# Attention feeding an MLP on one core: q and k loaded by casting DMA in six-token runs, with a drained first batch and a new load order

## The chip, the cores and the metric

The kernel runs on one core of a Trainium2 chip. The metric is the device time of one execution in microseconds (us). The profile of an execution gives each engine's instructions: TensorE (PE, and PEld for its weight loads), VectorE (DVE), ScalarE (ACT), GpSimd (POOL) and the queue of SyncE (SPq) that issues DMAs. PEclk is the clock that TensorE was granted, as a share of full speed. PSUM holds TensorE's results; to evacuate is to copy them out of it. A pair's step is the time from its first scores matmul to that of the next pair. The page's span is 1.6 to 2.1 us shorter than the time of the same run; where I subtract milestones of two traces, I use spans.

## The reference, cut to what matters

```python
# q, k, v: (8, 8, 576, 64) float32: batch, head, sequence, head_dim
scores = 0.125 * q @ k^T + slope[h] * (-(i - j))       # only where 0 <= i - j < 128
x = (softmax(scores) @ v).transpose(0, 2, 1, 3).reshape(4608, 512)
h = x @ w_in                                           # 512 x 2048
out = (h * clip(h + 3, 0, 6) / 6) @ w_out              # 2048 x 512
```

The kernel works through 32 head pairs (four to a batch, pair 0 to pair 31). For each it transposes q and k, makes the scores, exponentiates, masks, multiplies by v, normalizes and transposes back into `xT`. The MLP (called MoE in the code) follows in 288 "units": 144 up units (one 128x512 piece of h) and 144 down units, each of four matmuls of 512 columns. A token block's up units can start when all pairs of the batches it touches have come back. They are put between the steps of later pairs, to fill TensorE.

## The kernel before

Only TensorE's order is fixed by the program. The order on the other engines is chosen when the kernel is built, and in the traces VectorE and GpSimd then work through it in that order (below, copies whose data had landed at 5.8 and 7.5 us run at 20.3 us, behind another instruction).

```python
ps_tp = ...tile_pool(name="ps_tp", bufs=2, space=PSUM)   # one tag "tp": q, k and back share two buffers
...
def load_pair(got, b, hp):              # batch 0; float32, 256 B runs, from SyncE
    for nm, src in srcs:                # q, k, v
        for h in (2 * hp, 2 * hp + 1):
            nc.sync.dma_start(out=got[nm][:, 0:4, h, :],
                              in_=src[b, h, 0:512, :].rearrange("(t p) d -> p t d", p=128))
            ...
def cast_all(got, b):                   # batches 1 to 7: GpSimd casts q, k, v to bf16
    ...
def transposes(g):
    b, hp = divmod(g, NP)
    for src, nm in ((qbuf[b % 2], "qT"), (kbuf[b % 2], "kT")):
        tp = ps_tp.tile([128, SP], BF16, tag="tp", name="tp")
        for j in range(NQ):             # five 128x128 blocks
            nc.tensor.transpose(tp[:, ts(j, 128)], src[:, j, ts(hp, 128)], ident)
        t = qkt.tile([128, SP], BF16, tag=nm, name=nm)
        nc.vector.tensor_copy(out=t, in_=tp)
...
with tc.manual_schedule(engines={mybir.EngineType.PE}):
    prepare(0)
    transposes(0)
    for g in range(G + 1):              # fill(n): up to n MoE units
        scores_diag(g);  prepare(g + 1);  fill(2)
        values(g - 1, (0, 1, 2));         fill(1)
        values(g - 1, (3, 4));            fill(1)
        scores_off(g);                    fill(1)
        transposes(g + 1);                fill(1)
        back(g - 1);                      fill(2)
    fill(len(units))
```

(Guards for the first and last pair are cut.) w_in is loaded at pair 1's preparation and w_out at pair 3's, both by casting DMAs from GpSimd.

The softmax here doesn't subtract the row's maximum and nothing guards it: scores larger than these inputs give would overflow.

Of the kernel before, what the change touches and what calls it, by code (L numbers as in the profile page):

```python
# [18 lines left out]
def kernel(  # L19
# [38 lines left out]
    loads = ctx.enter_context(tc.tile_pool(name="loads", bufs=4))  # L58
# [3 lines left out]
    small = ctx.enter_context(tc.tile_pool(name="small", bufs=4))  # L62
# [5 lines left out]
    ps_tp = ctx.enter_context(tc.tile_pool(name="ps_tp", bufs=2, space=bass.MemoryType.PSUM))  # L68
# [3 lines left out]
    qbuf = [held.tile([128, NQ, H * D], BF16, name=f"qbuf{i}") for i in range(2)]  # L72
    kbuf = [held.tile([128, NQ, H * D], BF16, name=f"kbuf{i}") for i in range(2)]
    vbuf = [held.tile([128, NQ, H, W], BF16, name=f"vbuf{i}") for i in range(2)]
    p4buf = [held.tile([128, 2, 128], BF16, name=f"p4buf{i}") for i in range(2)]

    srcs = (("qf", q), ("kf", k), ("vf", v))

    def new_loads():
        return {nm: loads.tile([128, NQ, H, D], FP32, tag="ld", name=nm) for nm, _ in srcs}  # L80

    def load_pair(got, b, hp):
        for nm, src in srcs:
            for h in (2 * hp, 2 * hp + 1):
                nc.sync.dma_start(out=got[nm][:, 0:4, h, :],
                                  in_=src[b, h, 0:512, :].rearrange("(t p) d -> p t d", p=128))
                nc.sync.dma_start(out=got[nm][:LAST, 4, h, :], in_=src[b, h, 512:S, :])  # L87

    def load_all(got, b):
        for nm, src in srcs:  # L90
            for j in range(NQ):
                n = min(128, S - j * 128)
                nc.sync.dma_start(
                    out=got[nm][:n, j, :, :],
                    in_=src[b, :, ds(j * 128, n), :].rearrange("h p d -> p h d"))

    got0 = new_loads()
    for hp in range(NP):
        load_pair(got0, 0, hp)
# [10 lines left out]
    for i in range(2):  # L110
        nc.vector.memset(vbuf[i][:, :, :, D:W], 1.0)
        nc.vector.memset(vbuf[i][64:128, 4, :, 0:D], 0.0)
        nc.vector.memset(qbuf[i][64:128, 4, :], 0.0)
        nc.vector.memset(kbuf[i][64:128, 4, :], 0.0)
        nc.vector.memset(p4buf[i], 1.0)

    def load_weights_in():
        for g in range(4):
            nc.gpsimd.dma_start(
                out=w_in_sb[:, :, ts(g, 512)],  # L120
                in_=moe_w_in[:, ts(g, 512)].rearrange("(k p) f -> p k f", p=128))
# [7 lines left out]
    def cast_pair(got, b, hp, eng):  # L129
        for nm, dst in (("qf", qbuf[b % 2]), ("kf", kbuf[b % 2])):  # L130
            s = got[nm].rearrange("p j h d -> p j (h d)")
            eng.tensor_copy(out=dst[:, 0:4, ts(hp, 128)], in_=s[:, 0:4, ts(hp, 128)])  # L132
            eng.tensor_copy(out=dst[:LAST, 4, ts(hp, 128)], in_=s[:LAST, 4, ts(hp, 128)])
        hs = slice(2 * hp, 2 * hp + 2)
        vb = vbuf[b % 2]
        eng.tensor_copy(out=vb[:, 0:4, hs, 0:D], in_=got["vf"][:, 0:4, hs, :])
        eng.tensor_copy(out=vb[:LAST, 4, hs, 0:D], in_=got["vf"][:LAST, 4, hs, :])

    def cast_all(got, b):
        for nm, dst in (("qf", qbuf[b % 2]), ("kf", kbuf[b % 2])):  # L140
            s = got[nm].rearrange("p j h d -> p j (h d)")
            nc.gpsimd.tensor_copy(out=dst[:, 0:4, :], in_=s[:, 0:4, :])
            nc.gpsimd.tensor_copy(out=dst[:LAST, 4, :], in_=s[:LAST, 4, :])
        vb = vbuf[b % 2]
        nc.gpsimd.tensor_copy(out=vb[:, 0:4, :, 0:D].rearrange("p j h d -> p (j h) d"),
                              in_=got["vf"][:, 0:4, :, :].rearrange("p j h d -> p (j h) d"))
        nc.gpsimd.tensor_copy(out=vb[:LAST, 4, :, 0:D], in_=got["vf"][:LAST, 4, :, :])
# [3 lines left out]
    def transposes(g):  # L151
        b, hp = divmod(g, NP)
        for src, nm in ((qbuf[b % 2], "qT"), (kbuf[b % 2], "kT")):
            tp = ps_tp.tile([128, SP], BF16, tag="tp", name="tp")
            for j in range(NQ):
                nc.tensor.transpose(tp[:, ts(j, 128)], src[:, j, ts(hp, 128)], ident)  # L156
            t = qkt.tile([128, SP], BF16, tag=nm, name=nm)
            nc.vector.tensor_copy(out=t, in_=tp)  # L158
            st[g, nm] = t
# [75 lines left out]
    def back(g):  # L235
        b, hp = divmod(g, NP)
        avs = st[g, "avs"]
        tp = ps_tp.tile([128, SP], BF16, tag="tp", name="tp")
        for j in range(NQ):
            nc.tensor.transpose(tp[:, ts(j, 128)],  # L240
                                avs[:, j, :, :].rearrange("p e d -> p (e d)"), ident)
        nc.vector.tensor_copy(out=xT[:, hp, ds(b * S, S)], in_=tp[:, 0:S])  # L242
        done[0] = g + 1
# [33 lines left out]
    units = []  # L277
    for nt in range(n_nt + 1):
        for step in range(16):
            if nt < n_nt:  # L280
                units.append((nt, moe_up, step))
            if nt > 0:
                units.append((nt, moe_down, step))
    at = [0]

    def fill(n):
        for _ in range(n):
            if at[0] == len(units):
                return
            nt, fn, step = units[at[0]]  # L290
            if fn is moe_up and done[0] < NP * (min((nt * NT + NT - 1) // S, B - 1) + 1):
                return
            fn(nt if fn is moe_up else nt - 1, step)
            at[0] += 1

    G = B * NP
    got = {0: got0}

    def prepare(g):
        b, hp = divmod(g, NP)  # L300
        if b == 0:
            cast_pair(got[0], 0, hp, nc.vector)
            if hp == 1:
                load_weights_in()
            if hp == 3:
                load_weights_out()
        elif hp == 0:
            cast_all(got[b], b)
        if hp == 1 and b + 1 < B:
            got[b + 1] = new_loads()  # L310
            load_all(got[b + 1], b + 1)

    with tc.manual_schedule(engines={mybir.EngineType.PE}):
        prepare(0)
        transposes(0)
        for g in range(G + 1):
            if g < G:
                scores_diag(g)
            if g + 1 < G:
                prepare(g + 1)  # L320
            fill(2)
            if g > 0:
                values(g - 1, (0, 1, 2))
            fill(1)
            if g > 0:
                values(g - 1, (3, 4))
            fill(1)
            if g < G:
                scores_off(g)
            fill(1)  # L330
            if g + 1 < G:
                transposes(g + 1)
            fill(1)
            if g > 0:
                back(g - 1)
            fill(2)
        fill(len(units))
# [30 lines left out]
```

## Time and profile before

| | before |
|---|---|
| time, median of the first 3 runs | 418.05 us (417.54 to 421.3) |
| first scores matmul (pair 0) | 18.8 us |
| pair 4's scores | 63.7 us |
| first up matmul | 69.2 us |
| pair 9's scores | 103.2 us |
| step of a pair, pairs 10 to 31, mean | 9.99 us |
| span (profiled run, 419.74 us) | 417.7 us |

These are the lines of the page that matter: engine totals (busy us, share, instructions), then busy tenths in 40 slices of the span, for TensorE, its granted clock and the DMA engines.

```profile
span 417.7 us, 7115 instructions
PE 338.9 (81%) x2739; PEld 175.2 (42%) x2784; DVE 201.5 (48%) x438; ACT 198.5 (48%) x355; POOL 145.1 (35%) x217
...
PE   0141618878999899989998999899899999999985
PEclk9999999998999999999999999999999999999999
DMA  8989799997157989898470000001000000101011
```

The first six slices (63 us) are mostly empty on TensorE, while DMA is nearly full. After the tenth slice TensorE is the limit. The timeline (start, duration, engine, line, operation, output from inputs, count, idle time before it and what ended it) shows how the first stage ends:

```profile
62.30 0.84 PE L156 MATMUL tp<-ident,kbuf 128*128 128x128 bf16 x5 [4.07 <-POOL kbuf L142]
...
63.73 0.61 PE L168 MATMUL sc<-qT,kT 64*128 64x128 bf16 x8
...
69.19 2.60 PE L253 MATMUL hps<-xT,w_in_sb 128*128 128x512 bf16 x7 [0.22 <-issue]
```

The k transposes of pair 4 (batch 1) wait for GpSimd's cast of batch 1. Pair 3's back-transposes stand behind them in TensorE's order, and the first up unit needs pair 3. In the second stage, the transposes of a pair look like this:

```profile
209.00 0.44 PE L156 MATMUL tp<-ident,qbuf 128*128 128x128 bf16 x5
...
209.28 0.44 PE L156 MATMUL tp<-ident,kbuf 128*128 128x128 bf16 x5
209.48 0.49 DVE L158 COPY qT<-tp 128x640 bf16<-128x640 bf16 x1 [1.26 <-PE tp L156]
```

k's transposes start right after q's, while q's evacuation on VectorE has not begun.

### The profile page before, as it was taken

To read this page: it belongs to the slowest core of one execution; us is meant where nothing else is said; L and a number is where in the kernel's file an instruction comes from. 1 tells how busy PE (TensorE), PEld (TensorE's weight loads), DVE (VectorE), ACT (ScalarE), POOL (GpSimd) and SP (SyncE) were. 2 spreads that over 40 slices of the span, in tenths; PEclk is the share of its full clock that TensorE was granted. 3 is DMA by queue.
4 is the path that set the end of the run, shared out by engine and by line. 5 is a ranking of instruction groups with operands and counts; after the bars stand their busy time and mean duration, and the time that the engine had idled before them with its cause. 6 is when DMAs were issued, how large, how long until landed. Compare 5 with 4: busy or idle time off the path is not lost.

```text
span 417.7 us, 7115 instructions
## 1 busy us (share of the span) xinstructions
PE 338.9 (81%) x2739; PEld 175.2 (42%) x2784; DVE 201.5 (48%) x438; ACT 198.5 (48%) x355; POOL 145.1 (35%) x217
## 2 busy tenths in 40 slices
PE   0141618878999899989998999899899999999985
PEld 0021415445444444444454444444444444444432
DVE  3341614675455555555555555555555454344400
ACT  0240414675655565555565655556565534443400
POOL 3070464458657427342752374222222200000000
PEclk9999999998999999999999999999999999999999
DMA  8989799997157989898470000001000000101011
GB/s 134 195 148 199 151 198 197 209 201 135 49 132 166 179 176 166 161 186 152 116 163 25 27 26 27 27 27 39 32 31 27 27 25 30 48 25 52 25 70 55
DMA packets 122481, 42.40 MB, mean 101 GB/s; under 512 B 113744, under 2 KB 117840, under 8 KB 122448
## 3 DMA queue, kind: packets, MB, share of 16 engines
q1 hardware_dynamic: 118224, 37.76, 44.3%
q0 software_dynamic: 4224, 4.19, 6.2%
q8 instruction: 21, 0.34, 0.4%
q14 instruction: 12, 0.10, 0.1%
HBM read 36.70 MB, written 9.44 MB: 110 GB/s over the span
## 4 chain that ended last, share of the span: by engine, by line
PE 46%; DVE 15%; ACT 14%; issue 11%; DMA 8%; SPq 4%; POOL 1%; DVEq 0%; POOLq 0%; ACTq 0%
PE ops L267 22%; PE hps L253 13%; ACT r L257 8%; DMA vf<-in_v_dram 6%; DVE g L258 5%; DVE avs L231 4%; DVE osb L274 3%; ACT pd L173 3%; PE tp L156 2%; PE sc L168 2%; PE av L222 2%; PE sc L189 2%; ACT p4buf L202 2%; SPq L87 2%; DMA kf<-in_k_dram 2%
## 5 line engine op out<-in xcount | busy, mean ns | idle before, releaser
L258 DVE SCALAR_TENSOR_TENSOR g<-r,hps 128x512 bf16<-128x512 f32 x144 | 99.0, 687 | 117.0 <-ACT r L257 116.9
L253 PE MATMUL hps<-xT,w_in_sb 128*128 128x512 bf16 x535 | 144.4, 382 | 10.5 <-DVE xT L242 5.3
L267 PE MATMUL ops<-w_out_sb,g 128*128 128x512 bf16 x572 | 145.2, 379 | 5.6 <-DVE osb L274 3.1
L257 ACT ACTIVATE r<-hps,bias 128x512 f32<-128x512 f32 x144 | 99.2, 691 | 96.8 <-PE hps L253 93.9
L267 PEld LDWEIGHTS <-g 128*128 128x128 bf16 x576 | 53.6, 98 | 70.0 <-issue 15.1
L176 POOL TENSOR_SCALAR_AFFINE_SELECT pd<-pd 128x512 bf16<-128x512 bf16 x64 | 39.8, 644 | 96.9 <-ACT pd L173 96.9
L253 PEld LDWEIGHTS <-w_in_sb 128*128 128x128 bf16 x576 | 49.8, 98 | 49.9 <-issue 4.1
L204 POOL TENSOR_SCALAR_AFFINE_SELECT po<-po 128x512 bf16<-128x512 bf16 x64 | 40.4, 634 | 79.0 <-ACT po L199 75.7
L199 ACT ACTIVATE po<-sc,bias_o 128x512 bf16<-128x512 f32 x64 | 44.0, 687 | 39.3 <-PE sc L193 39.3
L173 ACT ACTIVATE pd<-sc,bias_d 128x512 bf16<-128x512 f32 x64 | 40.5, 683 | 43.1 <-PE sc L168 43.1
L222 PE MATMUL av<-vbuf,po 128*128 128x65 bf16 x256 | 26.1, 201 | 15.4 <-DVE avs L231 15.3
L158 DVE COPY qT<-tp 128x640 bf16<-128x640 bf16 x32 | 15.7, 492 | 35.9 <-PE tp L156 35.8
L156 PE MATMUL tp<-ident,kbuf 128*128 128x128 bf16 x160 | 16.4, 239 | 20.0 <-DVE kbuf L132 15.9
L231 DVE TENSOR_TENSOR avs<-av,rc 128x384 bf16<-128x384 f32 x64 | 31.4, 491 | 2.0
L156 PE MATMUL tp<-ident,qbuf 128*128 128x128 bf16 x160 | 16.2, 238 | 19.5 <-DVE qbuf L132 15.2
L222 PEld LDWEIGHTS <-po 128*128 128x128 bf16 x256 | 18.9, 102 | 29.3 <-DVE avs L231 29.0
L225 PE MATMUL av<-vbuf,pd 128*128 128x65 bf16 x256 | 25.0, 201 | 0.0
L156 PEld LDWEIGHTS <-qbuf 128*128 128x128 bf16 x160 | 12.1, 105 | 26.2 <-DVE qbuf L132 15.5
L225 PEld LDWEIGHTS <-pd 128*128 128x128 bf16 x256 | 20.0, 101 | 7.2 <-issue 0.8
L156 PEld LDWEIGHTS <-kbuf 128*128 128x128 bf16 x160 | 11.4, 106 | 21.6 <-DVE kbuf L132 16.9
L202 ACT ACTIVATE p4buf<-sc,bias_d 128x64 bf16<-128x64 f32 x64 | 20.2, 315 | 0.0
L274 DVE COPY osb<-ops 128x512 f32<-128x512 f32 x18 | 12.3, 685 | 16.0 <-PE ops L267 16.0
(46 smaller groups left out, 231.8 us busy)
## 6 DMA issues: line engine op xcount, KB each, us to landing
out_dram<-osb SPq DMA_DIRECT2D x36, 256.0 KB, 2.0
qf<-in_q_dram SPq DMA_DIRECT2D x28, 256.0 KB, 4.9
kf<-in_k_dram SPq DMA_DIRECT2D x28, 256.0 KB, 5.1
vf<-in_v_dram SPq DMA_DIRECT2D x28, 256.0 KB, 4.9
w_in_sb<-in_moe_w_in_dram POOLq DMA_DIRECT2D x4, 512.0 KB, 10.4
w_out_sb<-in_moe_w_out_dram POOLq DMA_DIRECT2D x4, 512.0 KB, 10.1
qf<-in_q_dram SPq DMA_DIRECT2D x15, 128.0 KB, 5.3
kf<-in_k_dram SPq DMA_DIRECT2D x15, 128.0 KB, 4.8
```

Of the source, the lines that this page charges most:

```text
L156: nc.tensor.transpose(tp[:, ts(j, 128)], src[:, j, ts(hp, 128)], ident)
L173: nc.scalar.activation(out=pd[:, e, :, :].rearrange("p j c -> p (j c)"), in_=sc[:, e, :], func=ACT.Exp, bias=bias_d[:, h:h + 1], scale=scale)
L176: nc.gpsimd.affine_select(out=pd[:, e, :, :], in_=pd[:, e, :, :], pattern=[[0, 4], [1, 128]], channel_multiplier=-1, base=0, compare_op=AL ...
L199: nc.scalar.activation(out=po[:, e, :, :].rearrange("p j c -> p (j c)"), in_=sc[:, e, :], func=ACT.Exp, bias=bias_o[:, h:h + 1], scale=scale)
L204: nc.gpsimd.affine_select(out=po[:, e, :, :], in_=po[:, e, :, :], pattern=[[0, 4], [-1, 128]], channel_multiplier=1, base=-1, compare_op=A ...
L222: nc.tensor.matmul(av[:, i, e, :], lhsT=po[:, e, qt - 1, :], rhs=vb[:, qt - 1, h, :], start=True, stop=False)
L225: nc.tensor.matmul(av[:, i, e, :], lhsT=d, rhs=vb[:, qt, h, :], start=(qt == 0), stop=True)
L231: nc.vector.tensor_tensor(out=st[g, "avs"][:, qts[0]:qts[0] + nq, :, :], in0=av[:, 0:nq, :, 0:D], in1=rc[:, 0:nq, :, :].to_broadcast([128, ...
L253: nc.tensor.matmul(hps, lhsT=w_in_sb[:, ks, ts(ms, 128)], rhs=xT[:, ks, ts(nt, NT)], start=(ks == 0), stop=(ks == n_ks - 1))
L257: nc.scalar.activation(out=r6, in_=hps, func=ACT.Relu, bias=bias3[:, 0:1], scale=1.0 / 6.0)
L258: nc.vector.scalar_tensor_tensor(out=gts[nt][:, ms, :], in0=r6, scalar=1.0, in1=hps, op0=ALU.min, op1=ALU.mult)
L267: nc.tensor.matmul(ops[nt, sub], lhsT=gts[nt][:, ms, ts(sub, 128)], rhs=w_out_sb[:, ms, :], start=(ms == 0), stop=(ms == n_ms - 1))
```

## The change

Its intent: fewer and larger DMA packets for q and k, no casts of them, and MoE work that starts as soon as batch 0 is finished. One partition takes six consecutive tokens of a head (1.5 KB of float32), and the DMA casts to bf16. VectorE gathers the two heads of a pair (`pr`), six 96-row transposes follow, and the evacuation puts the tokens back in order. Batch 0 is run to its end before batch 1's transposes; ten up units follow, then batch 1 with one unit a step, then the fills of before. The core of the diff:

```diff
-    ps_tp = ctx.enter_context(tc.tile_pool(name="ps_tp", bufs=2, space=bass.MemoryType.PSUM))
+    ps_tp = ctx.enter_context(tc.tile_pool(name="ps_tp", bufs=1, space=bass.MemoryType.PSUM))
+    def load_qk(b, hs):
+        for n, src in enumerate((q, k)):
+            nc.gpsimd.dma_start(
+                out=qkbuf[b % 2][n][:, hs, :],
+                in_=src[b, hs, :, :].rearrange("h (p t) d -> p h (t d)", t=RT))     # RT = 6
...
+        for n, nm in enumerate(("qT", "kT")):                # in transposes(g)
+            src = st.pop((g, n))
+            tp = ps_tp.tile([128, RT, RP], BF16, tag="tp", name="tp")
+            for t in range(RT):
+                nc.tensor.transpose(tp[:, t, :], src[:, t, :], ident[:RP, :RP])      # RP = 96
...
+            nc.vector.tensor_copy(out=dst[:, 0:S].rearrange("p (a t) -> p a t", t=RT),
+                                  in_=tp.rearrange("p t a -> p a t"))
...
-        tp = ps_tp.tile([128, SP], BF16, tag="tp", name="tp")   # in back(g)
+        tp = ps_tp.tile([128, SP], BF16, tag="tb", name="tb")
...
+        for n in range(2):                                   # in prepare(g)
+            pr = small.tile([RP, RT, 2 * D], BF16, tag=f"pr{n}", name="pr")
+            nc.vector.tensor_copy(
+                out=pr.rearrange("p t (e d) -> p e t d", e=2),
+                in_=qkbuf[b % 2][n][:, hs, :].rearrange("p e (t d) -> p e t d", t=RT))
+            st[g, n] = pr
+        if b < 2:
+            cast_v(vfs[b], b, hs, nc.vector)                 # v still comes as float32 from SyncE
+        elif hp == 0:
+            for i in range(NP):
+                cast_v(vfs[b], b, slice(2 * i, 2 * i + 2), nc.gpsimd)
...
+            if g == 2:                                       # end of the step of pair g
+                prefetch(1)
+                load_weights_out()
...
+        segment(0, NP, lambda g: (0,) * 6)                   # batch 0, no units, to its end
+        fill(10)
+        segment(NP, G, lambda g: (0, 0, 1, 0, 0, 0) if g < 2 * NP else (2, 1, 1, 1, 1, 2))
```

The pools of loads and small tiles shrink as well (from four buffers to two, and from four to three). The order of the MoE units changes with it: all 16 up units of block 0 and eight of block 1 come first. Just before pair 9's scores, both schedules have 18 units behind them.

More of the change, by code (lines that the diff above doesn't have):

```diff
@@ L56 @@
     bias_o = perm.tile([128, H], FP32)
-    loads = ctx.enter_context(tc.tile_pool(name="loads", bufs=4))
+    loads = ctx.enter_context(tc.tile_pool(name="loads", bufs=2))
     held = ctx.enter_context(tc.tile_pool(name="held", bufs=1))
@@ L61 @@
     ppool = ctx.enter_context(tc.tile_pool(name="ppool", bufs=3))
-    small = ctx.enter_context(tc.tile_pool(name="small", bufs=4))
+    small = ctx.enter_context(tc.tile_pool(name="small", bufs=3))
     gpool = ctx.enter_context(tc.tile_pool(name="gpool", bufs=2))
@@ L67 @@
     ps_av = ctx.enter_context(tc.tile_pool(name="ps_av", bufs=1, space=bass.MemoryType.PSUM))
-    ps_tp = ctx.enter_context(tc.tile_pool(name="ps_tp", bufs=2, space=bass.MemoryType.PSUM))
+    ps_tp = ctx.enter_context(tc.tile_pool(name="ps_tp", bufs=1, space=bass.MemoryType.PSUM))
     ps_h = ctx.enter_context(tc.tile_pool(name="ps_h", bufs=2, space=bass.MemoryType.PSUM))
     ps_o = ctx.enter_context(tc.tile_pool(name="ps_o", bufs=1, space=bass.MemoryType.PSUM))
-    qbuf = [held.tile([128, NQ, H * D], BF16, name=f"qbuf{i}") for i in range(2)]
@@ L73 @@
-    kbuf = [held.tile([128, NQ, H * D], BF16, name=f"kbuf{i}") for i in range(2)]
+    RP, RT = 96, 6
+    qkbuf = [[held.tile([RP, H, RT * D], BF16, name=f"qkbuf{n}{i}") for n in range(2)]
+             for i in range(2)]
     vbuf = [held.tile([128, NQ, H, W], BF16, name=f"vbuf{i}") for i in range(2)]
     p4buf = [held.tile([128, 2, 128], BF16, name=f"p4buf{i}") for i in range(2)]
-    srcs = (("qf", q), ("kf", k), ("vf", v))
-    def new_loads():
-        return {nm: loads.tile([128, NQ, H, D], FP32, tag="ld", name=nm) for nm, _ in srcs}
@@ L82, in load_pair @@
-    def load_pair(got, b, hp):
-        for nm, src in srcs:
-            for h in (2 * hp, 2 * hp + 1):
-                nc.sync.dma_start(out=got[nm][:, 0:4, h, :],
-                                  in_=src[b, h, 0:512, :].rearrange("(t p) d -> p t d", p=128))
-                nc.sync.dma_start(out=got[nm][:LAST, 4, h, :], in_=src[b, h, 512:S, :])
-    def load_all(got, b):
-        for nm, src in srcs:
-            for j in range(NQ):
-                n = min(128, S - j * 128)
-                nc.sync.dma_start(
-                    out=got[nm][:n, j, :, :],
-                    in_=src[b, :, ds(j * 128, n), :].rearrange("h p d -> p h d"))
@@ L97, with load_v_pair @@
-    got0 = new_loads()
-    for hp in range(NP):
-        load_pair(got0, 0, hp)
+    NKT = 3
+    kTbuf = [held.tile([128, SP], BF16, name=f"kTbuf{i}") for i in range(NKT)]
+    def load_qk(b, hs):
[3 more added lines that the diff above has]
+                in_=src[b, hs, :, :].rearrange("h (p t) d -> p h (t d)", t=RT))
+    def load_v_pair(vf, b, hp):
+        for h in (2 * hp, 2 * hp + 1):
+            nc.sync.dma_start(out=vf[:, 0:4, h, :],
+                              in_=v[b, h, 0:512, :].rearrange("(t p) d -> p t d", p=128))
+        if hp == 0:
+            nc.sync.dma_start(out=vf[:LAST, 4, :, :],
+                              in_=v[b, :, 512:S, :].rearrange("h p d -> p h d"))
@@ L101, with load_v, new_v @@
+    def load_v(vf, b):
+        for j in range(NQ):
+            n = min(128, S - j * 128)
+            nc.sync.dma_start(
+                out=vf[:n, j, :, :],
+                in_=v[b, :, ds(j * 128, n), :].rearrange("h p d -> p h d"))
+    def new_v():
+        return loads.tile([128, NQ, H, D], FP32, tag="ld", name="vf")
     make_identity(nc, ident)
@@ L112 @@
         nc.vector.memset(vbuf[i][64:128, 4, :, 0:D], 0.0)
-        nc.vector.memset(qbuf[i][64:128, 4, :], 0.0)
-        nc.vector.memset(kbuf[i][64:128, 4, :], 0.0)
         nc.vector.memset(p4buf[i], 1.0)
+    for t in kTbuf:
+        nc.vector.memset(t[:, S:SP], 0.0)
     def load_weights_in():
@@ L127, in load_weights_out, with cast_v @@
                 in_=moe_w_out[ds(g * 512, 512), :].rearrange("(m p) d -> p m d", p=128))
-    def cast_pair(got, b, hp, eng):
-        for nm, dst in (("qf", qbuf[b % 2]), ("kf", kbuf[b % 2])):
-            s = got[nm].rearrange("p j h d -> p j (h d)")
-            eng.tensor_copy(out=dst[:, 0:4, ts(hp, 128)], in_=s[:, 0:4, ts(hp, 128)])
-            eng.tensor_copy(out=dst[:LAST, 4, ts(hp, 128)], in_=s[:LAST, 4, ts(hp, 128)])
-        hs = slice(2 * hp, 2 * hp + 2)
-        vb = vbuf[b % 2]
-        eng.tensor_copy(out=vb[:, 0:4, hs, 0:D], in_=got["vf"][:, 0:4, hs, :])
-        eng.tensor_copy(out=vb[:LAST, 4, hs, 0:D], in_=got["vf"][:LAST, 4, hs, :])
-    def cast_all(got, b):
-        for nm, dst in (("qf", qbuf[b % 2]), ("kf", kbuf[b % 2])):
-            s = got[nm].rearrange("p j h d -> p j (h d)")
-            nc.gpsimd.tensor_copy(out=dst[:, 0:4, :], in_=s[:, 0:4, :])
-            nc.gpsimd.tensor_copy(out=dst[:LAST, 4, :], in_=s[:LAST, 4, :])
-        vb = vbuf[b % 2]
-        nc.gpsimd.tensor_copy(out=vb[:, 0:4, :, 0:D].rearrange("p j h d -> p (j h) d"),
-                              in_=got["vf"][:, 0:4, :, :].rearrange("p j h d -> p (j h) d"))
-        nc.gpsimd.tensor_copy(out=vb[:LAST, 4, :, 0:D], in_=got["vf"][:LAST, 4, :, :])
+    def cast_v(vf, b, hs, eng):
+        vb = vbuf[b % 2]
+        eng.tensor_copy(out=vb[:, 0:4, hs, 0:D], in_=vf[:, 0:4, hs, :])
+        eng.tensor_copy(out=vb[:LAST, 4, hs, 0:D], in_=vf[:LAST, 4, hs, :])
     st = {}
@@ L152, in transposes @@
         b, hp = divmod(g, NP)
-        for src, nm in ((qbuf[b % 2], "qT"), (kbuf[b % 2], "kT")):
-            tp = ps_tp.tile([128, SP], BF16, tag="tp", name="tp")
-            for j in range(NQ):
-                nc.tensor.transpose(tp[:, ts(j, 128)], src[:, j, ts(hp, 128)], ident)
-            t = qkt.tile([128, SP], BF16, tag=nm, name=nm)
-            nc.vector.tensor_copy(out=t, in_=tp)
-            st[g, nm] = t
+        for n, nm in enumerate(("qT", "kT")):
+            src = st.pop((g, n))
+            tp = ps_tp.tile([128, RT, RP], BF16, tag="tp", name="tp")
+            for t in range(RT):
+                nc.tensor.transpose(tp[:, t, :], src[:, t, :],
+                                    ident[:RP, :RP])
+            if n == 0:
+                dst = qkt.tile([128, S], BF16, tag="qT", name="qT")
+            else:
+                dst = kTbuf[g % NKT]
+            nc.vector.tensor_copy(out=dst[:, 0:S].rearrange("p (a t) -> p a t", t=RT),
+                                  in_=tp.rearrange("p t a -> p a t"))
+            st[g, nm] = dst
     def scores_diag(g):
@@ L237, in back @@
         avs = st[g, "avs"]
-        tp = ps_tp.tile([128, SP], BF16, tag="tp", name="tp")
+        tp = ps_tp.tile([128, SP], BF16, tag="tb", name="tb")
         for j in range(NQ):
@@ L275, in moe_down @@
             nc.sync.dma_start(out=out[ds(nt * NT + sub * 128, 128), :], in_=osb)
-    units = []
-    for nt in range(n_nt + 1):
+    units = [(0, moe_up, step) for step in range(16)]
+    units += [(1, moe_up, step) for step in range(8)]
+    for step in range(8):
+        units += [(1, moe_up, 8 + step), (1, moe_down, step)]
+    units += [(1, moe_down, 8 + step) for step in range(8)]
+    for nt in range(2, n_nt + 1):
         for step in range(16):
@@ L281 @@
                 units.append((nt, moe_up, step))
-            if nt > 0:
-                units.append((nt, moe_down, step))
+            units.append((nt, moe_down, step))
     at = [0]
@@ L296 @@
     G = B * NP
-    got = {0: got0}
+    vfs = {0: new_v()}
+    for hp in range(NP):
+        load_qk(0, slice(2 * hp, 2 * hp + 2))
+        load_v_pair(vfs[0], 0, hp)
+    load_weights_in()
     def prepare(g):
         b, hp = divmod(g, NP)
-        if b == 0:
-            cast_pair(got[0], 0, hp, nc.vector)
-            if hp == 1:
-                load_weights_in()
-            if hp == 3:
-                load_weights_out()
-        elif hp == 0:
-            cast_all(got[b], b)
-        if hp == 1 and b + 1 < B:
-            got[b + 1] = new_loads()
-            load_all(got[b + 1], b + 1)
@@ L313 @@
-    with tc.manual_schedule(engines={mybir.EngineType.PE}):
-        prepare(0)
-        transposes(0)
-        for g in range(G + 1):
-            if g < G:
-                scores_diag(g)
-            if g + 1 < G:
-                prepare(g + 1)
-            fill(2)
-            if g > 0:
-                values(g - 1, (0, 1, 2))
-            fill(1)
-            if g > 0:
-                values(g - 1, (3, 4))
-            fill(1)
-            if g < G:
-                scores_off(g)
-            fill(1)
-            if g + 1 < G:
-                transposes(g + 1)
-            fill(1)
-            if g > 0:
-                back(g - 1)
-            fill(2)
+        hs = slice(2 * hp, 2 * hp + 2)
@@ new lines, in prefetch, with segment @@
+    def prefetch(b):
+        vfs[b] = new_v()
+        if b == 1:
+            for hp in range(NP):
+                load_qk(b, slice(2 * hp, 2 * hp + 2))
+                load_v_pair(vfs[b], b, hp)
+        elif b < B:
+            load_qk(b, slice(0, H))
+            load_v(vfs[b], b)
+    def segment(lo, hi, fills):
+        prepare(lo)
+        transposes(lo)
+        for g in range(lo, hi + 1):
+            f = fills(g)
+            if g < hi:
+                scores_diag(g)
+            if g + 1 < hi:
+                prepare(g + 1)
+            fill(f[0])
+            if g > lo:
+                values(g - 1, (0, 1, 2))
+            fill(f[1])
+            if g > lo:
+                values(g - 1, (3, 4))
+            fill(f[2])
+            if g < hi:
+                scores_off(g)
+            fill(f[3])
+            if g + 1 < hi:
+                transposes(g + 1)
+            fill(f[4])
+            if g > lo:
+                back(g - 1)
+            fill(f[5])
+            if g == 2:
+                prefetch(1)
+                load_weights_out()
+            elif g % NP == 1 and g > NP and g // NP + 1 < B:
+                prefetch(g // NP + 1)
```

## The prediction

> **What bounds the kernel now.** Two stages. (1) Until 69.2 us (timeline, TensorE) no MoE matmul runs: the first up projection waits for batch 0's last back-transpose, which stands in TensorE's fixed order behind the transposes of batch 1, and those wait for batch 1's loads and casts (62.3 us). The page's second part shows the DMA engines 80 to 99% busy there: q, k, v go in 256 B packets (118,224 packets of queue 1 take 44.3% of 16 engines, 25 ns each), and w_in and w_out (98 ns per packet) are mixed into batch 0. (2) From about 100 to 395 us TensorE is the limit (windows: 18 to 19 of 20 us busy). A head-pair step with eight MoE units takes 9.99 us (scores of pair 9 at 103.2, of pair 31 at 322.9); by the waits it stalls some 0.7 us of that. The MoE-only tail follows.
>
> **What the change removes and adds.**
> - q and k: 768 packets of 1.5 KB instead of 4,608 of 256 B, per tensor and batch. Estimated at 75 to 98 ns each from w_in's 98 ns, a batch costs 14 to 16 us of the 16 engines instead of 21. GpSimd loses q and k casts (35 us, off the path).
> - Batch 0 is drained before any transpose of batch 1, so MoE starts when w_in and pair 3 are done. Estimate: first scores at 9 to 10 us, unfilled steps of 5.7 us (before: 5.0 to 5.8), drained at 35 us, ten up units at 1.28 us (two PSUM buffers; matmuls 0.87 + ACT 0.69 + DVE 0.69 + hops), pair 4's scores at 50, pair 9's at about 80 us against 103.2, with the same 18 MoE units done. Gain about 22 us.
> - VectorE: evacuations become strided PSUM reads. The Trainium skill, "VectorE: DVE Perf Modes", the perf-mode tier table and auto-detection, lets 16-bit step-1 data from PSUM run at 2x; with a stride it falls to 1x. Estimate from the 512-element fp32 PSUM copy (0.685 us): 0.75 us instead of 0.49. Plus two untangling copies a pair, about 0.36 us each. VectorE goes from 5.6 to some 6.9 us a step: not the limit.
> - TensorE: the transpose pool has one buffer for q and k where both had their own. k's transposes now wait for q's evacuation, with nothing between: q's transposes 0.3, pipe and semaphore 0.2, copy 0.75, semaphore 0.1, less issue: a new stall of about 1.0 us per pair, on the limiting engine. Over the 22 later steps: minus 22 us. Twelve 96-column transposes cost about what ten of 128 did.
>
> **On the critical path.** Start: nearly all of the 22 us. Steady: nearly all of the 1.0 us a step. They about cancel; the start may gain a little more than I count.
>
> **Prediction.** 416 us, range 402 to 430; faster 0.33, within 2% 0.47, slower 0.20.
>
> **What would show it.** First up matmul near 35 us (was 69.2); pair 9's scores near 80; step period near 10.9 us instead of 9.99; TensorE idle before k's transposes on the qT copy, about 1 us times 30, in groups and waits; strided copies near 0.75 us; casting packets at 75 to 98 ns.
>
> **What would make it wrong.** Faster: the k stall hides other stalls of the step (the 0.36 us on avs), or the start drains quicker. Slower: VectorE's order puts a product g ahead of the qT copy, so the stall is 1.5 to 2 us; v of batch 2, issued early, delays batch 1; descriptor writing on GpSimd is slow or held up behind mask selects, so batch 1 arrives after 50 us.

## The result, and the profile after

| | before | changed |
|---|---|---|
| time, median | 419.56 us (417.54 to 421.3, 4 runs) | 451.12 us (449.57 to 453.11, 4 runs) |
| first scores matmul | 18.8 us | 27.9 us |
| first up matmul | 69.2 us | 58.8 us |
| pair 4's scores | 63.7 us | 74.8 us |
| pair 9's scores | 103.2 us | 115.4 us |
| step, pairs 10 to 31 | 9.99 us | 10.84 us |
| span | 417.7 us | 450.0 us |

The changed kernel is slower: ratio 1.0757, 95% interval 1.068 to 1.0833. (A ratio here is the mean time of one kernel's fast runs over that of the other's of the same rounds, so it is not quite the ratio of the medians.)

The 32.3 us of span add up from milestones. Pair 9's scores come 12.2 us later. The step from pair 9 to 10 takes 11.7 us instead of 9.7, which adds 2.0. The next 21 steps lose 0.845 us each, together 17.7. The tail adds 0.4. So the start, which was to give 22 us, cost 12.

These are the same lines of the page as before:

```profile
span 450.0 us, 7218 instructions
PE 353.1 (78%) x2848; PEld 178.4 (40%) x2848; DVE 234.4 (52%) x493; ACT 199.5 (44%) x355; POOL 136.8 (30%) x251
...
PE   0024676677888888888888888888888899999975
PEclk9999998666899999999999999999999999999999
DMA  9999995508400940092017000000000001011011
```

TensorE is idle for two slices, is 20 to 79% busy up to the tenth, and never gets back to the 9s of before until the MoE-only tail. The clock row has a dip to 6 in slices 8 to 10 (79 to 113 us, so between pair 4 and pair 9) that was not there.

The start of the changed kernel, from the timeline of VectorE:

```profile
19.95 0.43 DVE L134 CAST vbuf<-vf 128x512 bf16<-128x512 f32 x1 [6.09 <-DMA vf<-in_v_dram]
20.30 0.89 DVE L305 COPY pr<-qkbuf 96x768 bf16<-96x768 bf16 x3
21.40 0.76 DVE L151 COPY qT<-tp 128x576 bf16<-128x576 bf16 x1 [0.21 <-PE tp L145]
...
26.72 0.43 DVE L134 CAST vbuf<-vf 128x512 bf16<-128x512 f32 x1 [4.03 <-DMA vf<-in_v_dram]
27.06 0.75 DVE L151 COPY kTbuf<-tp 128x576 bf16<-128x576 bf16 x1
```

TensorE in the same stretch:

```profile
20.70 0.66 PE L145 MATMUL tp<-ident,pr 96*128 96x96 bf16 x6 [20.70 <-DVE pr L305]
22.21 0.64 PE L145 MATMUL tp<-ident,pr 96*128 96x96 bf16 x6 [0.85 <-DVE qT L151]
27.87 0.61 PE L162 MATMUL sc<-qT,kTbuf 64*128 64x128 bf16 x8 [5.02 <-DVE kTbuf L151]
```

The `pr` copies run the moment a v cast has finished, and three run back to back: they were ready and waited for nothing of their own. That v cast had waited 6.09 us for v's DMA. The same happens again at 26.72 us: `kTbuf` for pair 0 stands behind a v cast of batch 1, which the scores of pair 0 do not need. The VectorE stream of the built kernel has the same order as the trace (not a profile; place in the stream, counted from 0 without semaphore instructions, line, instruction, what it is for or waits for):

```
10 L134 TensorCopy vbuf0<-vf 128x4x2x64 [v, pair 0]
...
15 L134 TensorCopy vbuf0<-vf 128x4x2x64 [v, pair 1]
...
33 L134 TensorCopy vbuf0<-vf 128x4x2x64 [v, pair 2]
34 L134 TensorCopy vbuf0<-vf 128x4x2x64 [v, pair 3]
35 L305 TensorCopy pr<-qkbuf00          [q, pair 0]
36 L305 TensorCopy pr<-qkbuf10          [k, pair 0]
...
41 L134 TensorCopy vbuf1<-vf            [v, batch 1]
42 L151 TensorCopy kTbuf0<-tp           [TensorE]
```

In the steady stage the transposes of a pair now look like this:

```profile
209.82 0.42 PE L145 MATMUL tp<-ident,pr 96*128 96x96 bf16 x6
...
210.28 0.76 DVE L151 COPY qT<-tp 128x576 bf16<-128x576 bf16 x1 [1.25 <-PE tp L145]
...
211.09 0.42 PE L145 MATMUL tp<-ident,pr 96*128 96x96 bf16 x6 [0.85 <-DVE qT L151]
```

k's six transposes wait 0.85 us for q's evacuation, because `tp` has one buffer. The groups of the page (busy us, mean ns, idle before and its cause) say it for the whole run:

```profile
L145 PE MATMUL tp<-ident,pr 96*128 96x96 bf16 x384 | 30.2, 221 | 49.6 <-DVE qT L151 28.9
...
L151 DVE COPY qT<-tp 128x576 bf16<-128x576 bf16 x32 | 24.2, 756 | 28.0 <-PE tp L145 28.0
```

28.9 us of TensorE idle time end with the qT copy, over 32 pairs. The copy takes 756 ns against 0.49 us before, although it moves fewer elements. The Trainium skill, "VectorE: DVE Perf Modes", the section on what auto-detection checks, gives 16-bit data its doubled rate only at unit step, and this trace agrees.

### The profile page after: what moved, and what is told of

It reads as the page before. It is cut to its first block, busy times and chain, and to the rows that moved or that the text cites. A ratio compares the mean times of both kernels' runs of the same rounds, so it can differ in the third digit from the quotient of the medians.

```text
span 450.0 us, 7218 instructions
## 1 busy us (share of the span) xinstructions
PE 353.1 (78%) x2848; PEld 178.4 (40%) x2848; DVE 234.4 (52%) x493; ACT 199.5 (44%) x355; POOL 136.8 (30%) x251
## 3 DMA queue, kind: packets, MB, share of 16 engines
q0 software_dynamic: 16960, 13.63, 20.7%
## 4 chain that ended last, share of the span: by engine, by line
PE 55%; DVE 20%; ACT 9%; issue 7%; SPq 6%; DMA 2%; POOL 0%; POOLq 0%; ACTq 0%; DVEq 0%
PE ops L261 22%; PE hps L247 19%; ACT r L251 6%; DVE g L252 6%; SPq L88 5%; DVE qT L151 5%; PE tp L145 4%; DVE avs L225 4%; PE sc L162 3%; PE av L216 2%; ACT pd L167 2%; DVE kTbuf L151 2%; DVE osb L268 2%; PE sc L183 2%; PE av L219 1%
## 5 line engine op out<-in xcount | busy, mean ns | idle before, releaser
L247 PE MATMUL hps<-xT,w_in_sb 128*128 128x512 bf16 x576 | 156.0, 396 | 5.5 <-DVE g L252 2.9
L261 PEld LDWEIGHTS <-g 128*128 128x128 bf16 x576 | 53.2, 97 | 67.6 <-issue 12.1
L247 PEld LDWEIGHTS <-w_in_sb 128*128 128x128 bf16 x576 | 51.4, 101 | 56.5 <-issue 12.2
L145 PE MATMUL tp<-ident,pr 96*128 96x96 bf16 x384 | 30.2, 221 | 49.6 <-DVE qT L151 28.9
L145 PEld LDWEIGHTS <-pr 96*128 96x128 bf16 x384 | 23.6, 106 | 59.3 <-issue 32.5
L216 PE MATMUL av<-vbuf,po 128*128 128x65 bf16 x256 | 26.7, 203 | 17.1 <-DVE avs L225 15.9
L151 DVE COPY qT<-tp 128x576 bf16<-128x576 bf16 x32 | 24.2, 756 | 28.0 <-PE tp L145 28.0
L305 DVE COPY pr<-qkbuf 96x768 bf16<-96x768 bf16 x64 | 25.4, 404 | 3.3 <-DMA qkbuf<-in_q_dram 2.9
L151 DVE COPY kTbuf<-tp 128x576 bf16<-128x576 bf16 x32 | 23.9, 748 | 2.9 <-PE tp L145 2.8
L134 POOL CAST vbuf<-vf 128x512 bf16<-128x512 f32 x24 | 14.8, 618 | 32.5 <-PE av L219 32.5
L162 PE MATMUL sc<-qT,kTbuf 64*128 64x128 bf16 x256 | 14.2, 237 | 12.9 <-DVE kTbuf L151 12.9
```

The source lines that it names most:

```text
L145: nc.tensor.transpose(tp[:, t, :], src[:, t, :], ident[:RP, :RP])
L151: nc.vector.tensor_copy(out=dst[:, 0:S].rearrange("p (a t) -> p a t", t=RT), in_=tp.rearrange("p t a -> p a t"))
L216: nc.tensor.matmul(av[:, i, e, :], lhsT=po[:, e, qt - 1, :], rhs=vb[:, qt - 1, h, :], start=True, stop=False)
L247: nc.tensor.matmul(hps, lhsT=w_in_sb[:, ks, ts(ms, 128)], rhs=xT[:, ks, ts(nt, NT)], start=(ks == 0), stop=(ks == n_ks - 1))
L261: nc.tensor.matmul(ops[nt, sub], lhsT=gts[nt][:, ms, ts(sub, 128)], rhs=w_out_sb[:, ms, :], start=(ms == 0), stop=(ms == n_ms - 1))
```

## The experiments

`tc.keep_in_program_order(ins)` adds an ordering edge only: `ins` may not be issued before what was written earlier for its engine. It adds no wait for data. All experiments gave correct results; each was timed against the kernel before in the same rounds.

Theory A for the start is VectorE's issue order. Rival B is the loads: casting DMA delivers q and k late. For the rest, the stall on `tp` and VectorE's added work compete, and later the drained schedule and the clock come in.

### 1. v casts of VectorE held in program order (vpin)

```diff
-        eng.tensor_copy(out=vb[:, 0:4, hs, 0:D], in_=vf[:, 0:4, hs, :])
-        eng.tensor_copy(out=vb[:LAST, 4, hs, 0:D], in_=vf[:LAST, 4, hs, :])
+        c1 = eng.tensor_copy(out=vb[:, 0:4, hs, 0:D], in_=vf[:, 0:4, hs, :])
+        pin(c1, eng)                     # tc.keep_in_program_order, if eng is VectorE
+        c2 = eng.tensor_copy(out=vb[:LAST, 4, hs, 0:D], in_=vf[:LAST, 4, hs, :])
+        pin(c2, eng)
```

> The changed kernel with one thing altered: the VectorE casts of v may not be issued ahead of VectorE instructions written earlier in the program. Theory A (the late start is VectorE's own issue order: v casts that wait for v's DMA stand in front of the first q and k copies, whose data have landed by about 8 us): the first scores matmul moves from 27.9 us to 10 to 14 us, and the run gets 8 to 18 us shorter than 450, about 432 to 442. Rival B (q and k themselves land late, the DMA is the cause): first scores stay after 20 us and the time stays within 3 us of 450. Neither touches the step period, 10.8 us.

Measured: 440.88 us (ratio to before 1.0481, interval 1.0425 to 1.0537). First scores at 12.1 us, step 10.84 us. Its timeline:

```profile
5.61 0.36 DVE L311 COPY pr<-qkbuf 96x768 bf16<-96x768 bf16 x1 [1.02 <-DMA qkbuf<-in_q_dram]
7.39 0.36 DVE L311 COPY pr<-qkbuf 96x768 bf16<-96x768 bf16 x1 [1.42 <-DMA qkbuf<-in_k_dram]
...
22.24 0.43 DVE L134 CAST vbuf<-vf 128x512 bf16<-128x512 f32 x1 [4.78 <-DMA vf<-in_v_dram]
...
22.71 0.74 DVE L157 COPY qT<-tp 128x576 bf16<-128x576 bf16 x1
```

q and k of pair 0 have landed at 5.6 and 7.4 us here, and at 5.8 and 7.5 us in the changed kernel's own trace. So rival B is out: the data were there 13 us before the changed kernel used them. The cure is partial. Pair 1's `qT` copy is still behind pair 3's v cast, and pair 1's scores come at 25.0 us.

### 2. Two transpose buffers again (twobuf)

```diff
-... tc.tile_pool(name="ps_tp", bufs=1, ...)
+... tc.tile_pool(name="ps_tp", bufs=2, ...)
-            tp = ps_tp.tile([128, RT, RP], BF16, tag="tp", name="tp")
+            tp = ps_tp.tile([128, SP], BF16, tag="tp", name="tp")
+            tp = tp[:, 0:S].rearrange("p (t a) -> p t a", t=RT)
-        tp = ps_tp.tile([128, SP], BF16, tag="tb", name="tb")    # back
+        tp = ps_tp.tile([128, SP], BF16, tag="tp", name="tp")
```

> The changed kernel with one thing altered: the transposes of q, of k and back share one tag with two PSUM buffers, as in the kernel before. Theory: the 0.85 us TensorE stall in front of k's transposes goes, the step period falls from 10.84 to 9.9 to 10.2 us, and the time by 15 to 20 us to 430 to 435. Rival (the period is up because of VectorE's added load, 1.2 us a step): the period stays above 10.5 and the time above 443. The start does not move: first scores about 27 us.

Measured: 430.77 us (ratio 1.0228, 1.0167 to 1.0289). The step falls from 10.84 to 10.13 us. First scores at 24.4 us.

```profile
208.93 0.68 PE L146 MATMUL tp<-ident,pr 96*128 96x96 bf16 x12
209.39 0.76 DVE L152 COPY qT<-tp 128x576 bf16<-128x576 bf16 x1 [1.25 <-PE tp L146]
209.45 1.03 PE L262 MATMUL ops<-w_out_sb,g 128*128 128x512 bf16 x4
```

Twelve transposes run in one piece and a down unit follows, while VectorE evacuates. So 0.71 of the 0.845 us a step were the missing buffer. The other 0.13 us remain with the strided copies and the `pr` copies; that VectorE's added load makes them is argued, not isolated.

### 3. Both, and the untangling copies held too (allpin_twobuf)

```diff
+            tc.keep_in_program_order(c)      # c: the pr copy; with the edits of vpin and twobuf
```

> Both alterations together, and the untangling copies of q and k also held in program order. If the start (theory A) and the stall are separate costs, they add: first scores 10 to 14 us, step period 9.9 to 10.2 us, time 405 to 422 us, about as the kernel before. If the DMA binds the start after all, 425 to 435.

Measured: 419.96 us, the same as before (0.9989, 0.9928 to 1.0051). First scores at 9.5 us and pair 3's at 26.2. But the first up matmul comes at 39.7 us (35 predicted), pair 4's scores at 57.1 and pair 9's at 98.3. One further case of an order that stops an engine showed up, on GpSimd:

```profile
61.41 0.62 POOL L134 CAST vbuf<-vf 128x512 bf16<-128x512 f32 x1 [22.97 <-DMA vf<-in_v_dram]
...
65.20 1.21 POOL L177 TENSOR_SCALAR_AFFINE_SELECT pd<-pd 128x512 bf16<-128x512 bf16 x2
...
65.89 0.24 PE L226 MATMUL av<-vbuf,pd 128*128 128x65 bf16 x1 [3.10 <-POOL pd L177]
```

Batch 2's v casts waited 23 us for their DMA and went ahead of pair 4's mask, for which TensorE waited 3.10 us. So pair 5 to pair 6 took 11.8 us.

### 4. The drained schedule alone, on the kernel before (drain_only)

The kernel before got the unit order, `segment`, `fill(10)`, the fills and the load order of the change; its loads, casts and transposes stay (VectorE casts batch 1 as well).

```diff
-    with tc.manual_schedule(engines={mybir.EngineType.PE}):
-        ... one loop over g, fills (2, 1, 1, 1, 1, 2)
+    with tc.manual_schedule(engines={mybir.EngineType.PE}):
+        segment(0, NP, lambda g: (0,) * 6)
+        fill(10)
+        segment(NP, G, lambda g: (0, 0, 1, 0, 0, 0) if g < 2 * NP else (2, 1, 1, 1, 1, 2))
```

> The kernel before with only the schedule of the change (batch 0 drained, load order b0, w_in, b1, w_out, same fills), and with its own loads, casts and transposes. Theory: draining is the useful part of the change; the first up projection comes at about 45 us instead of 69, pair 9's scores at 85 to 97 instead of 103, the period stays 9.99, and the time is 400 to 413 us. Rival (the drained schedule itself costs, since TensorE runs dry and its clock drops to half): 418 us or more.

Measured: 427.22 us, slower than before by 1.5% (1.0148, 1.0091 to 1.0204). My theory was wrong and the rival right. The first up matmul comes 12 us earlier (57.0 against 69.2 us), yet pair 9's scores come 5.6 us later (108.8 against 103.2). Its TensorE timeline holds two steps of the same kind, one after the other:

```profile
76.55 0.40 PE L168 MATMUL sc<-qT,kT 64*128 64x128 bf16 x8 [1.11 <-ACT p4buf L202]
...
79.42 1.90 PE L253 MATMUL hps<-xT,w_in_sb 128*128 128x512 bf16 x4
...
83.84 0.60 PE L168 MATMUL sc<-qT,kT 64*128 64x128 bf16 x8
...
86.25 1.03 PE L253 MATMUL hps<-xT,w_in_sb 128*128 128x512 bf16 x4
...
89.61 0.40 PE L168 MATMUL sc<-qT,kT 64*128 64x128 bf16 x8
```

The up unit takes 1.90 us in the first and 1.03 in the second, and the mean clock of the two steps is 0.62 and 0.89. The steps take 7.29 and 5.77 us. The prediction's 30 us from pair 4 to pair 9 are 6.0 a step, which only the second meets. One later wait is of another kind: in the step from pair 7 to 8 (9.97 us) pair 8's k transposes wait 3.41 us for GpSimd's cast of batch 2.

### 5. The drained schedule undone, on the changed kernel (undrain_only)

```diff
-        segment(0, NP, lambda g: (0,) * 6)
-        fill(10)
-        segment(NP, G, lambda g: (0, 0, 1, 0, 0, 0) if g < 2 * NP else (2, 1, 1, 1, 1, 2))
+        segment(0, G, lambda g: (2, 1, 1, 1, 1, 2))
```

(and the unit order of before)

> The changed kernel with only its schedule undone: one run through the 32 pairs with the fills of the kernel before, batch 0 not drained; its loads, its VectorE order and its single transpose buffer stay. Theory (draining is a loss in itself: it takes the up units away from the pairs of batch 1, which then run nearly unfilled, partly at half clock): first scores stay at 25 to 28 us, the period stays 10.8, but pair 9's scores come at 90 to 98 us instead of 115, and the time is 426 to 436 us. Rival (draining was right and only VectorE's order spoilt it): 446 us or more.

Measured: 438.49 us (1.0422, 1.0356 to 1.0488). Pair 9's scores come at 106.3 us, not at the 90 to 98 expected, since the first scores still come at 29.7 us. The direction holds: undoing the drain takes 10.6 us off the span (450.0 to 439.4) and 12.6 us off the median. The size expected was too large.

### 6. Casting loads with everything else undone or ordered (overlap_poolpin)

The edits of allpin_twobuf and undrain_only together, and the v casts on GpSimd held in program order as well.

> The casting loads and the strided evacuations kept, everything found harmful undone: two transpose buffers, v casts (VectorE and GpSimd) and untangling copies held in program order, and the schedule of the kernel before. If the costs found are separate: first scores 9.5 us, pair 4's about 33, first up projection 37 to 42, pair 9's scores 70 to 78, period 10.0 to 10.2, time 388 to 402 us. If DMA (w_in, then batch 1) binds: pair 9's scores 80 to 90 and 402 to 412 us.

Measured: **400.43 us, faster than the kernel before** (0.9521, 0.9469 to 0.9572). First scores 9.5 us, pair 4's 36.0, first up matmul 41.9, pair 9's scores 81.0, step 10.11 us. The page:

```profile
span 398.2 us, 7166 instructions
...
PE   1556786799998999898989898989899999999885
PEclk9999999599999999999999999999999999999999
DMA  9999999908350735064605300000000010010021
```

TensorE works from the first slice and is at 80% or more from the ninth to the MoE-only end. The time lies inside the range expected, near its end; pair 9's scores came at 81.0 us, later than the 70 to 78 expected and within the 80 to 90 of the DMA rival, so how far DMA binds this start stays open.

### 7. Idle matmuls to keep the clock up (warm)

```diff
+            if NP < g <= 2 * NP:
+                warm(5)          # behind values(g - 1, (0, 1, 2))
+            if NP < g < 2 * NP:
+                warm(2)          # in front of back(g - 1)
+    def warm(n):
+        scrap = ps_o.tile([128, d_model], FP32, tag="o", name="scrap")
+        for _ in range(n):
+            nc.tensor.matmul(scrap, lhsT=ident, rhs=w_in_sb[:, 0, 0:512], start=True, stop=True)
```

> As allpin_twobuf (drained schedule, 420 us), with idle matmuls into an unused PSUM bank put where TensorE waits in the steps of pairs 5 to 8 (five before the second half of the values, two before the back transposes); nothing reads them. Theory (the half clock makes these steps 7.3 us instead of 5.8): the clock stays full from 60 to 95 us, the steps fall to 5.7 to 6.3 us, and the time to 410 to 416 us. Rival (the steps are long for other reasons): the steps stay at 7 us or more, and the time is 419 or above.

Measured: 416.55 us (0.99, 0.9847 to 0.9952) where allpin_twobuf took 419.96. The clock was still at half through the first of these steps, which also holds GpSimd's wait of experiment 3 (13.8 us from pair 5 to 6); the next ones took 6.2 us against 7.4 and 7.1. This is inconclusive by time, so experiments 8 and 9 repeat it without GpSimd's wait.

### 8 and 9. The drain alone, and the clock alone (drained_allpin, drained_warm)

drained_allpin is overlap_poolpin with the drained schedule. drained_warm adds the idle matmuls and nothing else.

```diff
-        if eng is nc.vector:             # in pin(), on allpin_twobuf and on warm
-            tc.keep_in_program_order(ins)
+        tc.keep_in_program_order(ins)    # GpSimd's v casts too
```

> As overlap_poolpin in everything but the schedule, which is the drained one of the change. It makes the pair for the drain alone (overlap_poolpin took 400.4 us), and for drained_warm. Against allpin_twobuf (420.0) only GpSimd's v casts of batch 2 are held in program order; there pair 5 to pair 6 took 11.8 us with GpSimd in front of mask selects. Theory: that step falls to 7.0 to 7.8 us, time 414 to 417 us, so that draining alone costs 14 to 17 us. Rival: no gain from the order on GpSimd, 419 us or more.

> As drained_allpin with the idle matmuls of warm; the two differ in nothing else. Theory: the clock stays full in the steps of pairs 5 to 9, each falls from about 7.4 to 5.7 to 6.3 us, and the time is 4 to 7 us below drained_allpin. Rival (the half clock costs nothing): no difference beyond 1 us, or slower.

Measured: drained_allpin 412.87 us (0.9828, 0.9792 to 0.9864), drained_warm 410.83 us (0.977, 0.9734 to 0.9806). With order on GpSimd, the step from pair 5 to 6 is 7.3 us instead of 11.8. Against overlap_poolpin (400.43 us) the drain alone costs 12.4 us between medians of separate rounds, 14.2 us between spans (drained_allpin's is that of its slowest run). The next fences have the steps from pair 6 to 7 and from 7 to 8: busy us of TensorE, its weight loads, VectorE, ScalarE and GpSimd with instruction counts, then TensorE's granted clock, DMA share and GB/s. First drained_allpin:

```profile
69.00:76.50 7.50, 5.72 (x58) 3.66 (x57) 4.79 (x13) 3.52 (x7) 4.33 (x9) 0.50 0.73 97
76.50:83.80 7.30, 5.64 (x57) 3.67 (x57) 4.37 (x10) 3.52 (x7) 5.91 (x14) 0.50 1.28 221
```

Then drained_warm:

```profile
67.70:73.80 6.10, 4.89 (x63) 2.71 (x64) 4.58 (x13) 3.52 (x7) 4.18 (x8) 1.00 0.63 86
73.80:79.70 5.90, 4.80 (x65) 2.81 (x68) 4.36 (x11) 3.51 (x7) 4.90 (x12) 1.00 1.29 209
```

With more matmuls in them, the steps are shorter, 6.17 and 5.83 us from scores to scores instead of 7.44 and 7.32, at a clock of 1.00 instead of 0.50. The edit changes nothing else. Pair 4 to pair 9 takes 31.3 us instead of 36.9 in these two traces. In the timed runs the gain is smaller, 2.7 us between means (413.2 and 410.6), short of the 4 to 7 expected: the profiled run of drained_allpin had a mean clock of 0.961, its runs had 0.961 to 0.983 (mean 0.972), and drained_warm's had 0.985 to 0.996. How much of the first stage falls at half rate varies from run to run, and the two profiled runs happen to be the slowest of drained_allpin and the fastest of drained_warm, so their difference is larger than the usual one.

### 10. The load order alone, on the kernel before (before_wout_late)

```diff
-            if hp == 3:
-                load_weights_out()                       # batch 0, pair 3
         elif hp == 0:
             cast_all(got[b], b)
+            if b == 1:
+                load_weights_out()                       # behind batch 1's casts, held in order
```

> The kernel before with one thing altered: w_out is loaded after batch 1 instead of in front of it; loads, casts, transposes and fills stay. It asks how much of the gain of overlap_poolpin (400 us against 420) is the load order alone. If the 2.1 MB... of w_out in front of batch 1 cost what their packets take (4 x 512 KB, about 13 us of the 16 engines), the first up projection comes at 55 to 60 us instead of 69 and the time is 405 to 411 us. If the many small packets of batch 1 are the limit, it stays above 415.

Measured: 421.47 us, the same as before (1.0033, 0.9972 to 1.0093). The first up matmul does come 8.9 us earlier (60.3 us), but pair 9's scores come at 105.4 us, 2.2 later. An earlier first matmul is again not an earlier end, but its trace shows where the start is lost. Pair 7's scores still come 7.6 us earlier (84.3 against 91.9). Then:

```profile
87.86 1.89 POOL L146 CAST vbuf<-vf 128x2048 bf16<-128x2048 f32 x1 [2.64 <-DMA vf<-in_v_dram]
...
90.26 1.21 POOL L205 TENSOR_SCALAR_AFFINE_SELECT po<-po 128x512 bf16<-128x512 bf16 x2
...
90.94 0.24 PE L223 MATMUL av<-vbuf,po 128*128 128x65 bf16 x1 [5.46 <-POOL po L205]
```

A mask stands behind batch 2's v cast on GpSimd, as in experiment 3, and TensorE waits 5.46 us for it. From 84 to 105 us the clock is at 0.66 and then 0.51, where the kernel before had 0.79 to 1.00 from 83 to 103 us. Whether w_out, which now loads beside batch 2, made batch 2's data late was not isolated, so the run does not tell what the load order is worth with GpSimd's order mended. The expectation's volume should read 4.2 MB of float32, landing as 2.1 MB of bf16.

### 11. Fewer DMA issues for batch 1, on the best version (overlap_b1_halves)

```diff
             for hp in range(NP):
-                load_qk(b, slice(2 * hp, 2 * hp + 2))
+                if hp % 2 == 0:
+                    load_qk(b, slice(2 * hp, 2 * hp + 4))
...
             if g == 2:
                 prefetch(1)
+            elif g == 3:
                 load_weights_out()
```

> As overlap_poolpin, with batch 1's q and k in four DMAs of four heads instead of eight of two, and w_out's issues one pair later. There GpSimd waited 2.2 and 2.1 us at two of these issues (for w_in, whose completion counters are used again) while mask selects queued behind it, and pair 4's scores came at 36.0 us, 8.9 after pair 3's. Theory: the queueing goes, pair 4's scores come at 31 to 33.5 us, time 395 to 399 us. Rival (batch 1's data is what is late): 36 us or later and 400 us or more.

Measured: 401.57 us (0.9564, 0.9516 to 0.9612), pair 4's scores at 37.4 us: no gain, so the theory fell. GpSimd's two waits at these issues are gone, but batch 1's q and k now land later: VectorE waits 2.95 and 1.62 us for them (1.33 and 0.72 in overlap_poolpin), and since its `pr` copies are held in program order, the products that ended TensorE's next wait (5.75 us) stood behind them. An ordering edge can stop an engine too. overlap_poolpin stays the best version.

## Why the prediction was wrong

Spans and milestones side by side (us; all from profiled runs):

| | predicted | changed | allpin_twobuf | drained_allpin | drained_warm | overlap_poolpin | before |
|---|---|---|---|---|---|---|---|
| pair 0's scores | 9 to 10 | 27.9 | 9.5 | 9.5 | 9.5 | 9.5 | 18.8 |
| first up matmul | 35 | 58.8 | 39.7 | 39.7 | 39.6 | 41.9 | 69.2 |
| pair 4's scores | 50 | 74.8 | 57.1 | 56.5 | 56.7 | 36.0 | 63.7 |
| pair 9's scores | 80 | 115.4 | 98.3 | 93.5 | 88.0 | 81.0 | 103.2 |
| step, pairs 10 to 31 | 10.9 | 10.84 | 10.12 | 10.12 | 10.12 | 10.11 | 9.99 |
| span | | 450.0 | 417.3 | 412.5 | 407.0 | 398.2 | 417.7 |

**Right: the steady stage.** The new stall on k's transposes was there, at 0.85 us instead of 1.0, and the step was 10.84 us against 10.9 predicted. Strided copies took 0.75 us as estimated, the untangling copies 0.35 to 0.40. Casting packets cost what was estimated: queue 0 took 20.7% of 16 engines over 450 us for 16,960 packets; with the two weights' 4,224 at 98 ns taken off, that leaves 84 ns each. Experiment 2 shows the buffer as the cause.

**Wrong: the step "first scores at 9 to 10 us, unfilled steps of 5.7 us, drained at 35 us, ... pair 9's scores at about 80 us ... Gain about 22 us".** It came out as a loss of 12.2 us. The 35 us between 80 and 115.4 fall into parts:

- First scores came 18.4 us late (27.9 instead of 9.5). I took VectorE to run an instruction once its data are there. It runs its stream in a fixed order, and that order had v casts, whose DMAs landed at up to 20 us, in front of q and k copies whose data were in at 5.6 to 7.4 us. Experiments 1 and 3 show it: with ordering edges on the v casts alone the first scores come at 12.1 us, and with edges on the untangling copies and the second buffer as well at 9.5 us. I had named VectorE's order as a risk, but for a product in the steady stage, not here.
- From pair 0 to pair 3 it took 22.4 us, not 17.1: 5 us more. In allpin_twobuf this stretch took 16.7 us, so here the 5.7 us estimate was good and order was at fault again.
- From pair 3's scores to pair 4's it took 24.6 us, not 23.4. That it came out close is partly luck: in allpin_twobuf, with the order mended, the stretch took 30.9 us. There TensorE waited 4.26 us for pair 2's mask, which on GpSimd stood behind the issues of batch 1's loads, and two of these waited 2.02 and 2.10 us for w_in's DMA. Even drained_warm, with orders mended and the clock kept up, has pair 4's scores at 56.7 us, not 50, and pair 9's at 88.0, not 80.
- From pair 4 to pair 9 it took 40.6 us, not 30: 10.6 more. I had counted these thinly filled steps at full clock. TensorE was granted about half the clock for most of that stretch (the dip of the clock row; mean 0.64 from 75 to 115 us); in drained_allpin such a step took 7.3 to 7.4 us, and at full clock in drained_warm 5.8 to 6.2. Experiments 8 and 9 show the clock's share, 36.9 against 31.3 us in their traces (2.7 us between the means of the timed runs), and the two steps of experiment 4 agree with it within one trace. The other 3.7 us (40.6 against 36.9) go with what the changed kernel lacks beside drained_allpin, the second buffer and the order: k's transposes waited 4.9 us in all for qT copies there.

**Wrong in kind: that draining helps.** I read the wait of batch 0's back-transpose behind batch 1's loads as the thing to remove. With orders mended, the drained schedule (with its unit order) still costs 12.4 us (412.87 against 400.43); about 2.7 us of that are what experiment 9 gains by its clock. The ten up units run alone, one in 1.26 us for 0.87 us of matmuls (two PSUM buffers), and batch 1's pairs then run with nearly nothing between them. Undrained, the same 18 units are spread over those pairs' steps: from pair 3's scores to pair 9's it took 53.9 us in overlap_poolpin and 67.1 in drained_allpin.

**What stays open.** I did not isolate how much of overlap_poolpin's 20 us over the kernel before belongs to the casting loads and how much to the ordering edges; experiment 10 only rules out the load order of w_out as a sufficient cause. The last 0.13 us of the step is argued. What the load order of w_out is worth with GpSimd's order mended was not run.

## What to carry to other kernels

When a change adds instructions to an engine that serves several streams, read the built order of that engine, not only its load: one instruction waiting for a late DMA stops everything behind it, and an ordering edge was a cheap cure here (451.12 to 419.96 us with two buffers restored), though an edge in front of late data stops the engine as well (experiment 11). An earlier first matmul need not bring an earlier end, above all if the units that start then are taken from where they would have filled waits; compare a milestone behind the disturbed stretch, here pair 9's scores. Allow for half clock when you estimate a thinly filled TensorE stretch (here 7.3 to 7.4 us a step instead of 5.8 to 6.2, though not in every run), and give two transposes in a row two PSUM buffers (0.71 us a step here).

## What the Trainium skill lacked or had wrong

- "TensorE: Matmul & The Clock Gate", section "What's actually happening", lets the clock fall to half after at least one idle window of about 3.4 us. In drained_allpin it stayed at half from about 56 to 86 us although TensorE's longest wait between pair 4's scores and 86 us was 1.2 us, and 1.8 us just before. So in this kernel a thinly filled stretch without one long gap ran at half clock, which the section lacks. The page's later section on PSUM-queue depth-cycling has short idles make the clock swing between half and full, but no clock that stays at half. The half clock made a step of 5.8 to 6.2 us 7.3 to 7.4 us long; between the timed runs it was 2.7 us of 413. That the clock knows two values agrees (windows of 1.00 and 0.50 here).
- "VectorE: DVE Perf Modes", perf-mode tier table: no row for a strided 16-bit read from PSUM. The runs show 0.75 us for 576 elements a partition, against 0.49 us for 640 at unit step.
- "DMA: Bandwidth & Descriptors", section "Bandwidth": no figure for casting DMAs of middling runs. The runs show 84 ns a packet for 1.5 KB float32 runs landing as bf16, beside 25 ns for the 256 B packets of the kernel before.
- "Perfetto Trace Analysis", section "Identifying Dependency Chains", only tells to look at the semaphores that an instruction waits on. It lacks the instruction that is ready but stands behind another of its own engine. Here it shows as several copies back to back just after a wait of 6.09 us that was not theirs.
